# Two groups and an output turned by DMA, sink scores for two groups at once, scores in runs of three pairs, a table built later: one redesign of a windowed attention and its gated feed-forward block

## The chip, the cores and the metric

The kernel runs on one core of one Trainium2 chip. The metric is device microseconds of one execution, the median over several runs. Comparisons are made with runs of the kernel before on the same chip. Ratios are computed as the mean time of one kernel's fast runs over that of the other's fast runs of the same rounds, so a ratio is not quite the ratio of the medians quoted beside it. The profiled span is 1.7 us shorter than the timed one for the kernel before.

## The reference, cut to what matters

Attention of 4 batches, 8 heads, 768 positions, head width 64. Each query sees the last 128 positions and 4 "sink" positions at the start. The result, as 3072 tokens of width 512, goes through a gated feed-forward block of inner width 1536.

```python
keep = is_sink | in_window            # rel in [0, 128), or key < 4
a = softmax(where(keep, q @ k.T / 8, -1e9))
x = (a @ v) as [3072, 512]
g = x @ w_gate
out = (g * sigmoid(g) * (x @ w_val)) @ w_out
```

## The kernel before

The 3072 tokens are 12 groups of 256, three to a batch. For each group, queries and keys must be turned (head width on the partitions) before scores can be computed. Groups 0 to 3 are turned on TensorE (PE) by small matmuls against an identity; the others by the DMA crossbar, out of a loaded tile that is natural in layout.

```python
NPE = 4                               # groups below it are turned by TensorE
def step_T(g, ph): ...                # 32 transposes of 64x64, then two evictions
def cross_T(g):                       # on SyncE's queue
    for j in range(2):
        nc.sync.dma_start(t[:, j]..., nat[g][:, j]..., transpose=True)
```

The attention steps of a group are woven into the feed-forward work of earlier tokens, one unit at a time. A unit is one gate step (4 or 8 matmuls for `pg`, as many for `pv`) or one down tile (12 matmuls into `pd`). `slots` says which attention steps go into which unit. PE is given its instructions in this order; where the next one waits, it stands still. `S` are scores (`s`), `K` the scores against the sinks (`pk`), `PV` the product with the values (`o`), `X` a transpose of the attention output on PE (`px`), `C` a crossbar turn (`kqT`).

```python
def step_K(g):                        # sink scores of one group
    ...
    for p in range(NP2):
        nc.tensor.matmul(ps[KS*p:KS*(p+1)], kss[b][...],
                         queries(g, slice(0, P), p, 0, 2), ...)
us = [g0[0], held g0[2], alone, g0[2], *g1[0:3], g0[3], *g1[3:6], *g0[4:6],
      *downs(0), *g2, *downs(1), *downs(2)]
# ... cuts ...
(9, T(2)), ((10, 11), Ss(2)), (11, [K(2)]), ... (13, C(4)), ...
(15, T(3)), ((16, 17), Ss(3)), ... (18, C(5)), ((20, 21), Ss(4)), (21, [K(4)]),
((22, 22, 23, 23), PVs(4)), (24, Xs(4))
```

Loads are issued by GpSimd, at most eight in flight, in the order of the program: queries, keys, values and weights all share that one queue.

The softmax here doesn't subtract the row's maximum and nothing guards it: scores larger than these inputs give would overflow.

## Time and profile before

| | before |
|---|---|
| median of the timed runs | 245.19 us |
| profiled span | 243.4 us |
| TensorE busy | 96% |
| waits of TensorE for a transfer | none listed |
| first gate matmul | 18.06 us |
| first down matmul | 46.66 us |
| first gate matmul of block 3 | 80.89 us |

"Busy" counts the time in which an engine has an instruction under way; for TensorE, that is close to the whole span. The lines of the page, the waits and the orders of time on which the reasoning rests are in the prediction below. One view it did not look at is VectorE (DVE) in order of time just before the first gate. The columns are start, duration, instruction, and in brackets the idle time before it:

```profile
10.66 0.56 DVE L346 TENSOR_TENSOR e<-e,mask 128x768 bf16<-128x768 bf16 x1 [0.21 <-ACT e L341]
11.42 2.46 DVE L346 TENSOR_TENSOR e<-e,mask 128x768 bf16<-128x768 bf16 x2 [0.21 <-ACT e L341]
```

The same mask product of the same shape takes 0.56 us at 10.66 and 2.46 us for two right after it.

### The profile page before, as it was taken

How to read it: one execution, taken by the hardware profiler on the slowest of the kernel's cores; microseconds unless marked ns; L12 is line 12 of the kernel's file. 1: busy time of each engine (PE TensorE's matmuls, PEld its weight loads, DVE VectorE, ACT ScalarE, POOL GpSimd, SP SyncE). 2: the span in 40 equal slices, each digit the busy share in tenths (PEclk: the TensorE clock that was granted, in tenths of full speed). 3: DMA queues.
4: the chain of work that ended last, by engine and by line, in shares of the span. 5: the costliest groups of instructions: out<-in, count | busy, mean ns of one | idle time of the engine just before them, and what ended most of it. 6: DMA issues, size and time to landing. Idle time of an engine off the chain costs nothing.

```text
span 243.4 us, 5177 instructions
## 1 busy us (share of the span) xinstructions
PE 233.3 (96%) x2060; PEld 136.1 (56%) x2073; DVE 160.6 (66%) x336; ACT 111.2 (46%) x221; POOL 71.1 (29%) x92
## 2 busy tenths in 40 slices
PE   7779999999999999999999999999999999999994
PEld 2557887767755445554455454445454445488443
DVE  2688878929983489890598981399970489878100
ACT  2628637447471274532566512556612562232111
POOL 8985387794276814308000000000000000000000
PEclk9979999999999999999999999999999999999999
DMA  7999999999999999959930335900524200200132
GB/s 138 160 183 198 203 191 203 165 145 171 157 149 159 203 182 117 133 109 134 233 67 1 71 61 141 165 0 1 81 51 129 89 0 0 46 0 3 47 126 88
DMA packets 98792, 27.37 MB, mean 112 GB/s; under 512 B 84816, under 2 KB 95824, under 8 KB 98768
## 3 DMA queue, kind: packets, MB, share of 16 engines
q0 software_dynamic: 68832, 13.90, 70.2%
q1 hardware_dynamic: 29504, 12.75, 26.1%
q10 hardware_dynamic: 432, 0.39, 0.5%
q8 instruction: 16, 0.26, 0.4%
q14 instruction: 8, 0.07, 0.1%
HBM read 28.34 MB, written 6.29 MB: 142 GB/s over the span
## 4 chain that ended last, share of the span: by engine, by line
PE 87%; ACT 5%; DVE 5%; DMA 1%; issue 1%; DVEq 0%; ACTq 0%
PE pv L445 25%; PE pd L498 24%; PE pg L445 23%; PE o L381 5%; PE s L334 3%; ACT e L341 3%; PE pt L270 3%; DVE e L346 2%; PE wm L248 2%; DVE ht L460 1%; PE px L417 1%; DMA out_dram<-ot 1%; ACT xn L389 1%; DVE u L459 1%; ACT kT L275 0%
## 5 line engine op out<-in xcount | busy, mean ns | idle before, releaser
L445 PE MATMUL pv<-xT,wv 128*128 128x256 bf16 (+1 forms) x384 | 74.3, 326 | 0.9 <-DVE ht L460 0.9
L445 PE MATMUL pg<-xT,wg 128*128 128x256 bf16 (+1 forms) x384 | 74.2, 326 | 0.0
L452 ACT ACTIVATE th<-pg 128x512 f32<-128x512 f32 x72 | 43.7, 607 | 60.0 <-PE pg L445 59.4
L459 DVE SCALAR_TENSOR_TENSOR u<-th,pg 128x512 bf16<-128x512 f32 x72 | 49.2, 684 | 30.6 <-ACT th L452 30.1
L498 PE MATMUL pd<-wo,ht 128*128 128x512 bf16 x264 | 62.3, 379 | 0.6
L460 DVE TENSOR_TENSOR ht<-u,pv 128x512 bf16<-128x512 bf16 x72 | 49.5, 688 | 9.5 <-PE pv L445 2.9
L445 PEld LDWEIGHTS <-wg 128*128 128x128 bf16 x384 | 37.4, 98 | 25.4 <-issue 0.2
L341 ACT ACTIVATE e<-s 128x512 bf16<-128x512 f32 (+1 forms) x96 | 46.1, 582 | 0.9 <-PE s L334 0.8
L445 PEld LDWEIGHTS <-wv 128*128 128x128 bf16 x384 | 34.5, 97 | 21.0 <-issue 2.9
L498 PEld LDWEIGHTS <-ht 128*128 128x128 bf16 x276 | 25.8, 98 | 28.0 <-issue 0.2
L502 ACT ACTIVATE ot<-pd 128x512 f32<-128x512 f32 x23 | 13.7, 597 | 53.5 <-PE pd L498 53.5
L346 DVE TENSOR_TENSOR e<-e,mask 128x1024 bf16<-128x1024 bf16 (+1 forms) x48 | 30.4, 671 | 1.1 <-ACT e L341 0.9
L123 POOL DMA_DIRECT2D va<-in_v_dram x24 | 21.3, 894 | 6.0 <-DMA kq<-in_q_dram 3.3
L393 DVE TENSOR_TENSOR xn<-o,rcp 128x256 bf16<-128x256 f32 x46 | 19.5, 425 | 2.8 <-DMA xT<-xn 1.3
L107 POOL DMA_DIRECT2D kq<-in_k_dram x16 | 14.2, 887 | 23.8 <-DMA kqT<-kq 19.8
L381 PEld LDWEIGHTS <-e 128*128 128x128 bf16 x352 | 16.6, 98 | 7.9 <-DVE e L346 2.5
L381 PE MATMUL o<-va,e 128*128 128x65 bf16 x352 | 18.1, 195 | 2.2 <-DVE e L346 2.2
L107 POOL DMA_DIRECT2D kq<-in_q_dram x16 | 14.2, 888 | 6.4 <-DMA va<-in_v_dram 2.8
L386 DVE RECIPROCAL rcp<-o 128x4 f32<-128x4 f32 x48 | 8.4, 176 | 7.2 <-PE o L381 7.2
L275 DVE CAST qT<-pt 128x512 bf16<-128x512 f32 x7 | 4.6, 688 | 9.4 <-PE pt L270 9.4
L483 DVE TENSOR_SCALAR ot<-pd 128x256 f32<-128x256 f32 x1 | 0.4, 425 | 14.4 <-DMA out_dram<-ot 14.4
L381 PE MATMUL o<-vsb,es 128*128 128x260 bf16 x32 | 8.8, 275 | 0.8 <-ACT es L361 0.7
(61 smaller groups left out, 109.4 us busy)
## 6 DMA issues: line engine op xcount, KB each, us to landing
out_dram<-ot SPq DMA_DIRECT2D x23, 256.0 KB
va<-in_v_dram POOLq DMA_DIRECT2D x24, 128.0 KB, 9.1
kq<-in_k_dram POOLq DMA_DIRECT2D x18, 128.0 KB, 8.9
kq<-in_q_dram POOLq DMA_DIRECT2D x16, 128.0 KB, 9.2
wo<-in_moe_w_out_dram POOLq DMA_DIRECT2D x4, 384.0 KB, 12.4
wg<-in_moe_w_gate_dram POOLq DMA_DIRECT2D x4, 256.0 KB, 8.2
wv<-in_moe_w_val_dram POOLq DMA_DIRECT2D x4, 256.0 KB, 8.8
kq<-in_k_dram POOLq DMA_DIRECT2D x3, 256.0 KB, 9.0
```

Source lines behind the costliest of these rows:

```text
L107: nc.gpsimd.dma_start(x[:, j, i].rearrange("p (h d) -> p h d", d=D), src[b, :, t0:t0 + P].rearrange("h m d -> m h d"))
L123: nc.gpsimd.dma_start(va[:, j, :, 0:D], v[b, :, t0:t0 + P].rearrange("h m d -> m h d"))
L341: nc.scalar.activation(e_t[g][:, h0 + h, lo:512], pss[2 * pp + h][:, lo:512], AF.Exp, scale=scale)
L346: nc.vector.tensor_tensor(e, e, m[:, :, lo:512].broadcast_to([P, 2, 512 - lo]), op=ALU.mult)
L381: nc.tensor.matmul(o, l, r, start=(i == 0), stop=(i == len(mms) - 1), skip_group_check=True)
L393: nc.vector.tensor_tensor(xns[g, j][:, 256 * hh:256 * (hh + 1)].rearrange("p (h d) -> p h d", h=4), po[:, :, 0:D], rcp.broadcast_to([P, 4, ...
L445: nc.tensor.matmul(ps[:, i * n:(i + 1) * n], ws[fi][:, c, fo * P:(fo + 1) * P], x[:, 0:n // P, c], start=(c == 0), stop=(c == DMC - 1))
L452: nc.scalar.activation(th, pg, AF.Tanh, scale=0.5)
L459: nc.vector.scalar_tensor_tensor(u, th, 1.0, pg, op0=ALU.add, op1=ALU.mult)
L460: nc.vector.tensor_tensor(hts[tb][:, f:f + two].rearrange("p a n -> p (a n)"), u, pv, op=ALU.mult)
L498: nc.tensor.matmul(po, hts[tb][:, f, ts * P:(ts + 1) * P], wos[f // n][:, f % n], start=(f == 0), stop=(f == DFC - 1))
L502: nc.scalar.activation(ot, po, AF.Copy, scale=0.5)
```

## The change

The intent is to take work off TensorE, which bounds the kernel: turn groups 2 and 3 by the crossbar, turn group 4's attention output by DMA, score three head pairs in one visit to the 64-row form of the array instead of two, compute the sink scores of two groups together, and start the weight loads sooner by building the first sink table after them. The order of units was changed to match (block 1's down tiles before block 2's gates), and turns are issued sooner.

```diff
-    NPE = 4                 # turned by TensorE
-    NXPE = 5                # attention output turned by TensorE
+    NPE = 2
+    NXPE = 3
     load_v(1); load_gate(1)
-    build_vsb(0)
     for i in range(2, 5):
         load_gate(i)
+    build_vsb(0)
 def step_K(g):
+    n = 1 if g < GC else GC - c           # groups from g to the end of its batch
+    for i in range(n):
         ... queries(g + i, ...)
+def S3(ga, gb):                            # eight head pairs of two groups: 3, 3, 2
-    load4(2)
+    load1(2)                               # natural layout, for the crossbar
-    us = [..., *downs(0), *g2, *downs(1), *downs(2)]
+    us = [..., *downs(0), *downs(1), *g2, *downs(2)]
-    (9, T(2)), ((10, 11), Ss(2)), ... (15, T(3)), ((16, 17), Ss(3)), ...
+    (2, C(2)), (8, C(3)), ((11, 12), Ss(2)), (11, [K(2)]), ... (14, C(4)), ... (15, C(5)),
+    ((16, 18, 20), S3(3, 4)), (17, sinks(1)), ((17, 17, 19, 19), PVs(3)), (19, [K(4)]), ...
 # in the later weaves: S3 at s, s+3, s+6; K(7) at unit 1, K(10) at unit 5; turns C(8)..C(11) sooner
```
(Evictions, pool sizes and signatures are left out.)

More of the change, by code (lines that the diff above doesn't have):

```diff
@@ L64 @@
     vpool = pool("vpool", 1)
-    kqtp = pool("kqtp", 3)
+    kqtp = pool("kqtp", 2)
     crossp = pool("crossp", 4)
@@ L317, in step_ks, with step_S @@
                 else cross[b * GC][r, 0, 0, :, 0:NS])
-    def step_S(g, p2):
-        b, c = divmod(g, GC)
-        if p2 == 0:
-            e_t[g] = epool.tile([P, H, 512], BF16, tag="e", name="e")
-        parts = [(2 * c, 0, 2, P), (2 * c + 1, 1, 1, 3 * P)]
-        if c > 0:
-            parts.insert(0, (2 * c - 1, 0, 1, 0))
-        lo = 0 if c > 0 else P
-        pss = [bank([P, 512], FP32, "s") for _ in range(4)]
-        for pp in range(2):
-            p = 2 * p2 + pp
+    def step_S(*pairs):
+        runs = []
+        for g, p in pairs:
+            b, c = divmod(g, GC)
+            if p == 0:
+                e_t[g] = epool.tile([P, H, 512], BF16, tag="e", name="e")
+            parts = [(2 * c, 0, 2, P), (2 * c + 1, 1, 1, 3 * P)]
+            if c > 0:
+                parts.insert(0, (2 * c - 1, 0, 1, 0))
+            pss = [bank([P, 512], FP32, "s") for _ in range(2)]
+            runs.append((g, p, 0 if c > 0 else P, pss))
             for t, j, n, col in parts:
@@ L334, in step_S, with dve @@
                     nc.tensor.matmul(
-                        pss[2 * pp + h][:, col:col + n * P], keys(b, t, r, p),
+                        pss[h][:, col:col + n * P], keys(b, t, r, p),
                         queries(g, r, p, j, n), start=True, stop=True)
-        m = (mask if c > 0 else mask0).rearrange("q (o a) x -> q o (a x)", o=1)
-        for pp in range(2):
-            h0 = 4 * p2 + 2 * pp
+        for g, p, lo, pss in runs:
+            m = (mask if lo == 0 else mask0).rearrange("q (o a) x -> q o (a x)", o=1)
             for h in range(2):
                 nc.scalar.activation(
-                    e_t[g][:, h0 + h, lo:512], pss[2 * pp + h][:, lo:512],
+                    e_t[g][:, 2 * p + h, lo:512], pss[h][:, lo:512],
                     AF.Exp, scale=scale)
-            def dve(e=e_t[g][:, h0:h0 + 2, lo:512]):
+            def dve(e=e_t[g][:, 2 * p:2 * p + 2, lo:512], m=m, lo=lo):
                 nc.vector.tensor_tensor(
@@ L351, in step_K @@
         b, c = divmod(g, GC)
-        if c == 0:
-            return
-        ps = bank([P, 256], FP32, "pk")
-        for p in range(NP2):
-            nc.tensor.matmul(
-                ps[KS * p:KS * (p + 1)], kss[b][:, p * KS:(p + 1) * KS],
-                queries(g, slice(0, P), p, 0, 2), start=True, stop=True)
-        es_t[g] = espool.tile([P, 256], BF16, tag="es", name="es")
-        nc.scalar.activation(es_t[g], ps, AF.Exp, scale=scale)
+        n = 1 if g < GC else GC - c
+        ps = bank([P, n, 256], FP32, "pk")
+        for i in range(n):
+            for p in range(NP2):
+                nc.tensor.matmul(
+                    ps[KS * p:KS * (p + 1), i], kss[b][:, p * KS:(p + 1) * KS],
+                    queries(g + i, slice(0, P), p, 0, 2), start=True, stop=True)
+        es = espool.tile([P, 2, 256], BF16, tag="es", name="es")
+        nc.scalar.activation(es[:, 0:n], ps, AF.Exp, scale=scale)
+        for i in range(n):
+            es_t[g + i] = es[:, i]
     def step_PV(g, j, hh, act=False):
@@ L397, in step_PV @@
         later.append(dve)
-        if hh == 1 and (g >= NXPE or g == 3):
+        if hh == 1 and g >= NXPE:
             later.append(lambda: nc.sync.dma_start(
@@ L531, in Ss @@
     def Ss(g):
-        return [A(step_S, g, p2) for p2 in range(2)]
+        return [A(step_S, (g, p), (g, p + 1)) for p in (0, 2)]
+    def S3(ga, gb):
+        hs = [(ga, p) for p in range(NP2)] + [(gb, p) for p in range(NP2)]
+        return [A(step_S, *hs[i:i + 3]) for i in range(0, 2 * NP2, 3)]
     def PVs(g):
@@ L583 @@
     first_T(1)
-    step_S(0, 0)
+    step_S((0, 0), (0, 1))
     warm(1)
-    step_S(0, 1)
+    step_S((0, 2), (0, 3))
     warm(2)
@@ L600 @@
     step_ks(0)
-    step_S(1, 0)
-    load4(2)
+    step_S((1, 0), (1, 1))
+    load1(2)
     load_v(2)
@@ L621, in first_PVs @@
         later.extend(held)
-    us = [g0[0], (held_gate, 0, 2), (alone, 0, 0), g0[2], *g1[0:3], g0[3], *g1[3:6], *g0[4:6],
-          *downs(0), *g2, *downs(1), *downs(2)]
+    us = [g0[0], (held_gate, 0, 2), (alone, 0, 0), g0[2], *g1[0:3], g0[3], *g1[3:6],
+          *g0[4:6], *downs(0), *downs(1), *g2, *downs(2)]
     weave(us, slots(
-        (0, [flush, A(step_S, 1, 1), K(1), A(next_load, 1)]), (2, [first_PVs]),
-        (3, [A(step_X, 1, 0), A(step_X, 1, 1, True), flush]),
-        (9, T(2)), ((10, 11), Ss(2)), (11, [K(2)]),
-        (12, PVs(2)[:2] + [flush]), (13, PVs(2)[2:] + [flush]), (13, C(4)),
-        (14, [A(step_X, 2, 0), A(step_X, 2, 1, True), flush]),
-        (15, T(3)), ((16, 17), Ss(3)), (17, sinks(1)), ((18, 18, 19, 19), PVs(3)),
-        (18, C(5)), ((20, 21), Ss(4)), (21, [K(4)]),
-        ((22, 22, 23, 23), PVs(4)), (24, Xs(4))))
+        (0, [flush, A(step_S, (1, 2), (1, 3)), K(1), A(next_load, 1)]), (2, [first_PVs]),
+        (2, C(2)), (3, [A(step_X, 1, 0), A(step_X, 1, 1, True), flush]), (8, C(3)),
+        ((11, 12), Ss(2)), (11, [K(2)]), (13, PVs(2)[:2] + [flush]),
+        (14, PVs(2)[2:] + [flush]), (14, C(4)),
+        (15, [A(step_X, 2, 0), A(step_X, 2, 1, True), flush]),
+        (15, C(5)), ((16, 18, 20), S3(3, 4)), (17, sinks(1)), ((17, 17, 19, 19), PVs(3)),
+        (19, [K(4)]), ((21, 21, 22, 22), PVs(4))))
@@ L635, in pair @@
     def pair(ga, gb, sh=0):
         s = sh
-        return [((s, s + 2), Ss(ga)), (s + 2, [K(ga)]),
-                ((s + 4, s + 5, s + 6, s + 7), PVs(ga)),
-                ((s + 6, s + 8), Ss(gb)), (s + 8, [K(gb)]),
+        return [((s, s + 3, s + 6), S3(ga, gb)), ((s + 2, s + 4, s + 5, s + 7), PVs(ga)),
                 ((11, 11, 12, 12) if s else (10, 11, 12, 13), PVs(gb))]
     weave(gates(3) + downs(3), slots(
-        *pair(5, 6, 2), (2, C(6)), (10, C(7))))
-    weave(gates(4) + downs(4), slots((0, sinks(2)), *pair(7, 8), (3, C(8)), (10, C(9)), (14, C(10))))
@@ L645 @@
-    weave(gates(5) + downs(5), slots((0, sinks(3)), *pair(9, 10), (10, C(11))))
+        *pair(5, 6, 2), (2, C(6)), (10, C(7)), (14, C(8))))
+    weave(gates(4) + downs(4), slots(
+        (0, sinks(2)), *pair(7, 8), (1, [K(7)]), (5, C(9)), (10, C(10)), (14, C(11))))
+    weave(gates(5) + downs(5), slots(
+        (0, sinks(3)), *pair(9, 10), (5, [K(10)])))
     weave(gates(6) + gates(7) + downs(6) + downs(7), slots(
-        ((0, 2), Ss(11)), (2, [K(11)]), ((4, 5, 6, 7), PVs(11))))
+        ((0, 2), Ss(11)), ((4, 5, 6, 7), PVs(11))))
```

## The prediction

> **What bounds the kernel now.** I read the page first, then the waits of TensorE, then its instructions in order of time, then the DMA queues in stretches. The page's shares, its tenths in 40 slices (6.1 us each) and its chain:
>
> ```profile
> PE 233.3 (96%) x2060; PEld 136.1 (56%) x2073; DVE 160.6 (66%) x336; ACT 111.2 (46%) x221; POOL 71.1 (29%) x92
> ...
> PE   7779999999999999999999999999999999999994
> ...
> DMA  7999999999999999959930335900524200200132
> ...
> PE 87%; ACT 5%; DVE 5%; DMA 1%; issue 1%; DVEq 0%; ACTq 0%
> ```
>
> TensorE (PE) carries the end: from slice 4 (18 us) on it is never below 90%, and the chain is 87% PE. But the DMA row is just as full in slices 2 to 15, up to about 92 us, and sparse after that. So there are two limits: PE over the whole span, and in the first third a transfer stage which PE happens not to wait for. The waits of PE say so (line, what ended the wait, us in total, times, longest):
>
> ```profile
> PE o L381 <- DVE e L346: 2.2, 3, 1.1
> ...
> PE pv L445 <- DVE ht L460: 0.9, 3, 0.4
> ```
>
> Most of the first stands before 14 us, which the change leaves alone; no DMA is in the list. After 18 us PE stands still for only about 2 us in all, so what the change can gain is PE work, and what it can lose is a wait for DMA that now has none. What a piece of attention costs PE is read from the starts in its order of time (start, duration, instruction):
>
> ```profile
> 35.78 1.04 PE L445 MATMUL pg<-xT,wg 128*128 128x256 bf16 x8
> 36.75 1.09 PE L270 MATMUL pt<-ident,kq 64*64 64x64 bf16 x64
> 37.77 1.05 PE L445 MATMUL pv<-xT,wv 128*128 128x256 bf16 x8
> 38.65 1.04 PE L445 MATMUL pg<-xT,wg 128*128 128x256 bf16 x8
> 39.62 0.61 PE L334 MATMUL s<-qT,kT 64*128 64x128 bf16 x12
> 40.17 1.05 PE L445 MATMUL pv<-xT,wv 128*128 128x256 bf16 x8
> ```
>
> Undisturbed, pg to pv takes 0.87 us (37.77 to 38.65 is such a step). With the 64 transposes of group 2 between them it takes 1.99, so a group's turning costs 1.12. With one score run of two head pairs it takes 40.17 - 38.65 = 1.52, so a run costs 0.65. Its work is 2 x 0.21 (a pair is 512 columns on two half arrays at once; a 512-column matmul takes 0.216), so 0.22 of each run is going into the 64-row form and out of it.
>
> Now the transfers. POOL's queue is q0, the SyncE queue with crossbar turns and stores is q1. First q0 alone (stretch 40 to 52 us), then both (52 to 60 us); packets, MB, share:
>
> ```profile
> q0 software_dynamic: 11305, 1.97, 210.0%
> ```
>
> ```profile
> q0 software_dynamic: 4406, 0.56, 154.4%
> q1 hardware_dynamic: 2145, 0.59, 67.7%
> ```
>
> In the second stretch one group's keys and queries are turned: 2 x 1024 packets of 256 B. q0 with 128 B packets alone runs at about 1190 packets per us (the packets from 50 to 52 us), so 8 us would have carried 9,500; it carried 4,400. The turn thus cost the loads about 4.3 us of transfer. How long it took from its issue shows in SyncE's own order of time:
>
> ```profile
> 49.10 5.13 SPq L304 DMA_TRANSPOSE kqT<-kq  x2
> 54.33 1.10 SPq L504 DMA_DIRECT2D out_dram<-ot  x2
> 55.53 7.98 SPq L304 DMA_TRANSPOSE kqT<-kq  x2
> ```
>
> Its second half was issued as the load landed (50.8), and its last packets went at 59.4: 8.6 us later. The same pair of turns with q0 idle (106.6 to 109.2) took 2.6.
>
> **What the Trainium skill says.** "TensorEngine Tiling (Array Packing)", Key Properties: changing the tiling mode, not merely the tile, drains TensorE. The trace agrees: 0.22 per score run beyond its columns, about 0.11 each way. "DMA: Bandwidth & Descriptors", Queues, rings and completion order: each DMA engine goes round between the rows that have work, packet by packet. The trace agrees in kind: from 61.5 to 67 us q0 and q1 move the same number of packets, about 205 per half us each. Same page, Specifications: below 512 B a transfer is not at line rate. It agrees: 128 B packets land about 155 GB/s in SBUF, 512 and 1024 B ones about 200. Same page, Latency and other measured facts: DMA transposes at 261 GB/s with a non-contiguous middle dimension; here, with q0 idle, about 200.
>
> **The change part by part.**
> Groups 2 and 3 by the crossbar, group 4's attention output too: PE loses 2 x 1.12 = 2.24 us, and 2 x 0.22 = 0.43 for the eight 128-wide transposes of group 4. This is on the path. ACT and DVE lose the evictions (0.59 and 0.69 us each, four apiece); they are off it.
> Scores in runs of three pairs: 24 runs become 20, so 4 x 0.22 = 0.88 off PE.
> Sink scores for two groups at once: before, 8 runs of 0.22 behind a score run (42.57 to 42.79). After, two such runs, and three with twice the columns (0.21) that stand alone and pay both switches (0.22): 1.75 us either way. Nothing.
> First sink table later in POOL's order (1.30 us): loads wait for the landing of the eighth before them, weights land every 1.3 us before and after that instruction, and q0 never runs dry. Nothing.
> PE work removed: 2.24 + 0.43 + 0.88 = 3.55 us, 245.16 to 241.6.
> Added: a run of three takes 6 of 8 PSUM banks and puts six exponentials (0.58 each) in front of ACT's next tanh and es. Working one weave by hand with the trace's durations, es comes about 0.4 late and two banks 0.2 late where before a weave had 0.2 to 0.4 of such waits: about +0.3 each, +0.8 in all.
> Added on DMA: groups 2 and 3 load 128 B packets, four DMAs of 0.9 us in place of two of 1.4, +0.9 each; two turns at about 4.3 each; two smaller turns for group 4. Some 10 us more must pass before group 4 can be used, in the stage where DMA is full.
>
> When is each needed, if PE did not wait? Before, the gates' unit 11 starts at 41.05; without the group 2 transposes and one score run moved behind, at 39.3, and its scores of group 2 at **40.2**. Two units with scores, then four down tiles of 2.6 us with PV and transposes, put the first scores of group 3 at **55.3** and of group 4 at **60.7**.
> When do they arrive? The last weights land at 30.96; then four loads of 0.9: group 2 at 34.4 (before 33.6). Plus 8.6: turned at **43.0**, 2.8 late. If the 1024 B packets of w_out (16 engines, 201 per us) alternate with 256 B ones (590 per us), 150 pairs per us, it is rather 47. w_out itself, 42.9 before, lands at about 48 and is wanted from 44 plus the wait on: just in time.
> Group 3 lands at 45.55 + 1.8 + 4.2 = 51.5, turned at about 60, 4.7 late. Group 4 lands at 50.8 + 1.8 + 8.4 = 61, turned at 69.6, 8.9 late. If turns ran at their own speed and loads gave way, 50.8 + 1.8 + 3 x 3.5 (2048 packets at 590 per us) = 63, and with a start delay like the observed 2.9 us nearer 65: 4 late. These latenesses are not summed; the largest remains, as each pushes PE back and gives the next one time. Later groups have slack: group 5 was turned at 67.4 and used at 85.4.
> So PE waits 4 to 9 us between 40 and 80 us. I take 5, nearer the lower end, because units were moved (down tiles of the next block before gates, turns issued early) by someone who saw this limit. Sum: 245.16 - 3.55 + 0.8 + 5 = 247.4.
>
> **Rivals.**
> (a) The turns arrive in time: 245.16 - 3.55 + 0.8 = 242.4, or 241 if PE's small waits go too. For it: turns alone took 2.6 us, and packets were shared unevenly at times (from 54 to 55 us five to eight to one in favour of q1). Against: q0 is full without a gap to 92 us.
> (b) Turns take strict turns with w_out, and stores and group 4's small turns queue behind group 5's big ones, so gates of block 3 wait as well: 8 to 10 us of waiting, 250 to 251. For it: a store or turn on SyncE's queue took 3 to 4 us to start under load (67.4 to 71.8).
> (c) Three-pair runs starve PSUM: DVE is at 80 to 100% while PE runs gates with scores; if masks come late, each weave could lose 1 to 2 us, 244 to 246 without DMA waits. Against: by hand the banks come free in time.
>
> **Range and chances.** (a) gives the low end, (b) with some of (c) the high end: 242 to 252. Faster by over 2% means under 240.3, below the removed work itself: 0.07. Slower by over 2% needs over 250.1, a wait of about 8 us: 0.23. Within 2%: 0.70.
>
> **What would show it.** PE's transposes 64-wide: 160 in place of 288; score runs 20; PE busy about 4 us less. If right, PE's waits list the crossbar's kqT (or issue gaps before L334 scores) with 4 to 9 us in all between 40 and 65 us. Wrong if PE is at 90% in every slice from 18 us on (then rival a), or if its new waits name exponentials, masks or ht (then c), or xT (then b). The prologue to 18 us should be the same to 0.3 us, and POOL's landing of the weights too; if they land sooner, my zero for the sink table is wrong.

## The result

The changed kernel takes 271.00 us (270.31 to 271.77) against 245.19: ratio 1.107, interval 1.102 to 1.112. It is 10.7% slower, and the result is correct. The forecast was 247.4, within 242 to 252: the direction was right, and the loss was over ten times the one forecast. First the page of the changed kernel: busy shares, the tenths of PE, its granted clock and the DMA engines in 40 slices (6.7 us each), and the chain that ended last.

```profile
PE 238.0 (88%) x1924; PEld 135.9 (51%) x1937; DVE 157.1 (58%) x330; ACT 109.0 (41%) x214; POOL 75.0 (28%) x96
...
PE   7799980999839919999994999999999999999994
...
PEclk9979996699968968999997999999999999999999
DMA  8999999999999999962799114280030410100122
...
PE 52%; DMA 36%; POOL 3%; DVE 3%; issue 2%; ACT 1%; SPq 0%; POOLq 0%; DVEq 0%; ACTq 0%
```

Four holes stand in the PE row: slice 7, slices 11 and 12, slice 15, and slice 22. In or right after each, the clock row drops too. The chain, 1% DMA before, is now 36% DMA. What PE waited for:

```profile
PE s L334 <- DMA kqT<-kq: 8.3, 3, 5.5
PE pk L358 <- DMA kqT<-kq: 7.3, 2, 4.1
PE pg L448 <- DMA xT<-xn: 5.8, 1, 5.8
PE o L384 <- DVE e L345: 1.7, 4, 0.5
```

All three large waits are for transfers, which stood nowhere in this list before. In order of time, each with its idle time in brackets:

```profile
38.03 1.04 PE L448 MATMUL pg<-xT,wg 128*128 128x256 bf16 x8
44.57 0.29 PE L334 MATMUL s<-kqT,kT 64*128 64x128 bf16 x2 [5.50 <-DMA kqT<-kq]
47.31 0.50 PE L334 MATMUL s<-kqT 64*128 64x256 bf16 x4 [2.46 <-DMA kqT<-kq]
...
78.21 0.40 PE L358 MATMUL pk<-kqT,ks 128*32 128x256 bf16 x4 [4.05 <-DMA kqT<-kq]
...
100.09 1.87 PE L448 MATMUL pg<-xT,wg 128*128 128x512 bf16 x4 [5.78 <-DMA xT<-xn]
...
145.08 0.40 PE L358 MATMUL pk<-kqT,ks 128*32 128x256 bf16 x4 [3.25 <-DMA kqT<-kq]
```

The first two are the scores of group 2. The third and the fifth are sink scores: four matmuls for the first group of the pair run, then PE stands until the second group (5, and later 8) has been turned. The fourth is the first gate of block 3, which needs group 4's attention output. They add up to 5.50 + 2.46 + 4.05 + 5.78 + 3.25 = 21.0 us. Note also the 1.87 us of four 512-wide matmuls at 100.09: at full clock such a set takes 1.03.

Where the time went, by the first matmul of each part, from the two traces:

| stretch | before | after | difference |
|---|---|---|---|
| start to first gate | 18.06 | 16.57 | -1.49 |
| to first down tile | 28.60 | 37.01 | +8.41 |
| to block 3's gates | 34.23 | 46.51 | +12.28 |
| to block 4's gates | 35.84 | 37.65 | +1.81 |
| to block 5's gates | 37.24 | 41.74 | +4.50 |
| to the end | 89.45 | 89.55 | +0.10 |

From block 5's gates to the end the kernel is as before to 0.1 us. The loss lies in the stretches with the waits, and 1.81 us in the one to block 4's gates, which has no such wait but begins with work at half clock. The trace has four spells of half clock, each beginning within a wait, with 16.4 us of PE work inside. If half of that is lost, the books nearly close: 21.0 + 8.2 - 3.55 (the work removed) - 1.5 (the start) = 24.2 of 25.6 us.

Why was group 2's turn so late? The DMA queues from 36 to 42 us; columns are packets, MB, share:

```profile
q0 software_dynamic: 971, 0.95, 93.9%
q1 hardware_dynamic: 868, 0.22, 27.6%
```

q0 (loads) carries w_out here, in packets of 1024 B; q1 (the turn) carries 256 B at a time. They move nearly the same number of packets, so the turn gets a fifth of the bytes. Its packets start at 36.3 and end at 46.4 us by the trace: 10 us for what took 2.6 us with an idle q0. It was not issued late: SyncE issued its two halves at 32.38 and 34.06, as their loads landed (32.31 and 34.01).

### The profile page after: what moved, and what is told of

Its sections match the earlier page's. It is cut to its first block, busy times and chain, and to the rows that moved or that the text cites. A ratio compares the mean times of both kernels' runs of the same rounds, so it can differ in the third digit from the quotient of the medians.

```text
span 269.0 us, 4913 instructions
## 1 busy us (share of the span) xinstructions
PE 238.0 (88%) x1924; PEld 135.9 (51%) x1937; DVE 157.1 (58%) x330; ACT 109.0 (41%) x214; POOL 75.0 (28%) x96
## 4 chain that ended last, share of the span: by engine, by line
PE 52%; DMA 36%; POOL 3%; DVE 3%; issue 2%; ACT 1%; SPq 0%; POOLq 0%; DVEq 0%; ACTq 0%
PE pv L448 18%; PE pg L448 17%; DMA kq<-in_q_dram 14%; PE pd L501 13%; DMA kqT<-kq 8%; DMA xT<-xn 5%; DMA wo<-in_moe_w_out_dram 4%; PE o L384 3%; DMA wv<-in_moe_w_val_dram 3%; PE s L334 2%; DMA kq<-in_k_dram 1%; ACT e L340 1%; DVE ht L463 1%; DMA out_dram<-ot 1%; DVE u L462 1%
## 5 line engine op out<-in xcount | busy, mean ns | idle before, releaser
L448 PE MATMUL pg<-xT,wg 128*128 128x256 bf16 (+1 forms) x384 | 78.0, 339 | 5.8 <-DMA xT<-xn 5.8
L448 PE MATMUL pv<-xT,wv 128*128 128x256 bf16 (+1 forms) x384 | 77.7, 337 | 0.1
L455 ACT ACTIVATE th<-pg 128x512 f32<-128x512 f32 x72 | 43.7, 607 | 75.2 <-PE pg L448 72.3
L448 PEld LDWEIGHTS <-wg 128*128 128x128 bf16 x384 | 38.9, 102 | 33.9 <-issue 8.7
L448 PEld LDWEIGHTS <-wv 128*128 128x128 bf16 x384 | 35.4, 100 | 21.9 <-issue 4.7
L107 POOL DMA_DIRECT2D kq<-in_k_dram x20 | 17.9, 893 | 37.9 <-DMA kqT<-kq 31.6
L107 POOL DMA_DIRECT2D kq<-in_q_dram x20 | 17.7, 886 | 6.2 <-DMA kq<-in_q_dram 2.2
L334 PE MATMUL s<-kqT 64*128 64x256 bf16 (+1 forms) x208 | 12.6, 249 | 3.4 <-DMA kqT<-kq 2.8
L334 PEld LDWEIGHTS <-kqT 64*128 64x128 bf16 x208 | 7.6, 98 | 10.3 <-issue 10.0
## 6 DMA issues: line engine op xcount, KB each, us to landing
wo<-in_moe_w_out_dram POOLq DMA_DIRECT2D x4, 384.0 KB, 10.1
```

What stands on the lines that cost most here:

```text
L107: nc.gpsimd.dma_start(x[:, j, i].rearrange("p (h d) -> p h d", d=D), src[b, :, t0:t0 + P].rearrange("h m d -> m h d"))
L334: nc.tensor.matmul(pss[h][:, col:col + n * P], keys(b, t, r, p), queries(g, r, p, j, n), start=True, stop=True)
L448: nc.tensor.matmul(ps[:, i * n:(i + 1) * n], ws[fi][:, c, fo * P:(fo + 1) * P], x[:, 0:n // P, c], start=(c == 0), stop=(c == DMC - 1))
L455: nc.scalar.activation(th, pg, AF.Tanh, scale=0.5)
```

## The experiments

Twelve kernels ran on the chip; all gave correct results. First, three parts of the change, each alone on the kernel before. The order of units, the sink scores of two groups and the DMA for group 4's output were not tried alone on it.

**The sink table alone.**

```diff
-    build_vsb(0)
     for i in range(2, 5):
         load_gate(i)
+    build_vsb(0)
```

> The kernel before with one edit: the first sink table is built on GpSimd behind all weight loads. On record I valued this at zero. The changed kernel's trace shows its first gate matmul at 16.57 us against 18.06 before, and before that two mask products of 1.13 and 1.41 us in place of 0.56 each, at the time when GpSimd builds the table (12.16 to 13.46). Theory: the table's build and VectorE's products slow each other, and moving it gives 1.2 to 1.6 us: 243.7 to 244.0, mask products 0.56 each, first gate matmul near 16.6. Rival: only the weights come sooner, which nobody waits for: 245.2, first gate matmul at 18.0.

Measured: 243.72 us against 244.25, ratio 0.998 (0.995 to 1.001): not clear of zero. The profile of this run shows why both sides of the expectation held something. On its VectorE, in order of time, the two products that were slow in the kernel before are now as short as the others:

```profile
11.20 0.56 DVE L346 TENSOR_TENSOR e<-e,mask 128x768 bf16<-128x768 bf16 x1 [0.21 <-ACT e L341]
11.96 0.56 DVE L346 TENSOR_TENSOR e<-e,mask 128x768 bf16<-128x768 bf16 x1 [0.21 <-ACT e L341]
```

In this run the first gate matmul came at 16.11 us instead of 18.06. But PE then found a new wait, which the kernel before does not have:

```profile
PE pv L445 <- DMA wv<-in_moe_w_val_dram: 1.3, 1, 1.3
```

So 1.3 of the 1.95 us went straight into waiting for the second weight block. Nor are the 1.95 us the table's alone: the slow products explain 1.1 (2.46 us in place of the 1.32 from 11.20 to 12.52), and the kernel before had a half-clock spell of 3.4 us from 14.03, which this run did not have.

**Table late, and group 1's values behind that weight block**, to remove the new wait:

```diff
-    load_v(1)
     load_gate(1)
-    build_vsb(0)
+    load_v(1)
     ...
+    build_vsb(0)
```

> The kernel before with the first sink table behind the weights, as in the run of that alone, and group 1's values loaded behind the second weight block. In that run 1.3 us of the 1.95 gained came back as a wait for the second block's value weights at 21 us. Theory: that wait goes (the block lands 1.7 us sooner, group 1's values about 2.6 later, at 20.3, wanted at 22.5): 242.3 to 242.9, faster than before by 0.6 to 1.0%. Rival: the wait moves to group 1's values or to the third block of weights: 243.5 to 244.

Measured: 243.73 against 244.36, ratio 0.998 (0.995 to 1.002). The wait for weights is gone from the list, but the gain did not grow: this profile has the first gate at 17.25 us, partly because a half-clock spell of 3.4 us (14.5 to 17.9) fell on the work before it, while the profile of the table alone had none there. The expectation of 0.6 to 1.0% fell. The prologue varies by about as much as the edit is worth.

**Runs of three alone**, in the three later weaves, sink scores still per group:

```diff
-    ((s, s + 2), Ss(ga)), (s + 2, [K(ga)]), ((s + 4, ..., s + 7), PVs(ga)),
-    ((s + 6, s + 8), Ss(gb)), (s + 8, [K(gb)]), ...
+    ((s, s + 3, s + 6), S3(ga, gb)), (s + 1, [K(ga)]), (s + 6, [K(gb)]),
+    ((s + 2, s + 4, s + 5, s + 7), PVs(ga)), ...
```

> The kernel before with score runs of three head pairs in the three paired weaves only (groups 5 and 6, 7 and 8, 9 and 10), sink scores still per group, group 8 turned one half weave sooner because its scores come sooner. Theory: three runs fewer at 0.22 us, three sink runs standing alone at +0.11, waits for sink exponentials up to 0.4 each: 244.5 to 246, no wait over 0.6 us. Rival (PSUM starved by six banks at once): waits of 1 to 2 us per weave for masks or exponentials, 248 to 250.

Measured: 248.18 against 244.25, ratio 1.015 (1.011 to 1.019): slower than the theory allowed, and not for the rival's reason. The waits name a transfer, 1.85 us of it for group 6 and 0.89 for group 8:

```profile
PE s L334 <- DMA kqT<-kq: 2.7, 2, 1.8
```

The second run of a weave takes two of its three pairs from the second group, so that group's turned keys are wanted three units sooner.

**The same, with those turns issued sooner** (C(6) during block 2's down tiles, C(7) and C(8) at units 8 and 12 of block 3):

> The run of three-pair score runs alone, with the crossbar turns of groups 6, 7 and 8 issued two to four units sooner. In that run TensorE waited 1.85 and 0.89 us for turned keys (groups 6 and 8), of the 3.9 us by which it was slower. Theory: runs of three lose only because they ask for the second group's turned keys sooner; without those waits 244.0 to 245.5. Rival: ScalarE and PSUM under six exponentials in a row cost the rest, 246 to 247.5, with waits for exponentials or masks of over 0.5 us in each weave.

Measured: 245.84 against 244.91, ratio 1.004 (1.001 to 1.008). No wait for a transfer is left, and the median lies just above the theory's range; no wait of the weaves reaches 0.5 us, so the rival's picture doesn't hold either. Runs of three are thus no gain here, though they save 0.66 us of switching by the prediction's count. What takes it back, sink scores that stand alone or small waits, was not measured apart. Most of the 3.9 us of the run before was transfers asked for too soon.

**The crossbar for groups 2 and 3 alone**, with the order of units of before:

```diff
-    NPE = 4
+    NPE = 2
-    load4(2)
+    load1(2)
-    (9, T(2)), ... (15, T(3)),
+    (2, C(2)), (8, C(3)), ...
```

> The kernel before with groups 2 and 3 turned by the crossbar (turns issued at units 2 and 8 as in the change) and nothing else. Theory: the scores of group 2 are wanted at 38.5 us and the turned keys land at about 47.3 as in the changed kernel: a wait of 8 to 9 us, about 2.5 us more because TensorE's clock is halved after it, less 2.24 of transposes: 253 to 257. Rival: most of the changed kernel's loss comes from the other parts (sink scores of two groups, group 4's output turned by DMA, order of units), then 243 to 248.

Measured: 254.34 against 244.25, ratio 1.042 (1.038 to 1.045), inside the theory's 253 to 257. PE waits 10.6 us for group 2, for its two halves in turn:

```profile
PE s L334 <- DMA kqT<-kq: 10.6, 2, 7.8
```

Groups 3, 4 and 5 are in time in this run: once PE has been held back for group 2, nothing later is late. This is a large part of the loss, but 10 us of nearly 26.

Next, one part undone in the changed kernel.

**Sink scores for one group at a time.**

```diff
-    n = 1 if g < GC else GC - c
+    if c == 0: return                     # as before: one group
-    (1, [K(7)]), ... (5, [K(10)])
+    (s + 1, [K(ga)]), (s + 6, [K(gb)]), ... (2, [K(11)])
```

> The changed kernel with sink scores computed for one group at a time. Theory: computing them for two groups asks for the next group's turned queries too soon; without it the waits of 4.06 us (for group 5) and 3.25 us (for group 8) go, and with them 3.8 us of half-clock work; the wait for group 4's output (5.8) stays: 258 to 263. Rival: the waits only move to the next user of the crossbar (scores of group 8 two units later, group 4's output): 267 to 271.

Measured: 264.54, ratio 1.082 (1.079 to 1.086), against 1.107 of the changed kernel: 6.1 us less (2.5% of 244.3), somewhat less than expected. The waits at `pk` are gone and have not moved to group 8's scores; those for group 2 and for group 4's output have grown a little:

```profile
PE s L334 <- DMA kqT<-kq: 10.1, 3, 6.7
PE pg L444 <- DMA xT<-xn: 6.2, 1, 6.2
```

**Group 4's output by TensorE again.**

```diff
-        if hh == 1 and g >= NXPE:
+        if hh == 1 and (g >= 5 or g == 3):
-    ((21, 21, 22, 22), PVs(4))
+    ((21, 21, 22, 22), PVs(4)), (24, Xs(4))
```

> The changed kernel with group 4's attention output turned by TensorE again (eight 128-wide transposes, 0.43 us). Theory: the wait of 5.78 us before block 3's gates goes, with 1.7 us of half clock after it: 263 to 265. Rival: group 3's output, also turned by DMA behind the turn of group 5, ends the same wait: 268 to 271.

Measured: 266.45, ratio 1.091 (1.087 to 1.094): 4 us less than the changed kernel. The wait for xT is gone, so group 3's output was not what ended it; the rival falls. But the theory's number was too good, because the wait for group 8 grew from 3.25 to 5.15 us:

```profile
PE pk L358 <- DMA kqT<-kq: 9.8, 2, 5.2
```

**Idle matmuls in the waits**, to hold the clock:

```diff
-    ((11, 12), Ss(2)), ...
+    (11, [A(warm, 30)]), ((11, 12), Ss(2)), ...
+    (19, [A(warm, 25), K(4)]), ... warm(22) before block 3 ... (1, [A(warm, 11), K(7)])
```

> The changed kernel with idle 512-column matmuls on zeros put where TensorE waits for a transfer (30 before the scores of group 2, 25 before the sink scores of groups 4 and 5, 22 before block 3's gates, 11 before the sink scores of groups 7 and 8), at most as long as those waits. The result and all transfers stay as they are. Theory: each wait of over 3 us is followed by 3 to 5 us of work at half clock, 8 us lost in all; with TensorE kept at work the clock stays full. The 2.5 us after the first wait are given back in the next wait, which ends with a transfer, so 5 to 6 us are gained: 265 to 266, no half clock between 20 us and the end. Rival: the waits end with transfers that depend on one another alone, so the total stays: 270 to 272, though the clock is full.

Measured: 269.67, ratio 1.106 (1.101 to 1.111), where the changed kernel has 1.107: no difference clear of noise. The clock did what was meant:

```profile
PEclk9979999999999999999999999999999999999999
```

The total lies just under the rival's 270 to 272 and well above the theory's 265 to 266. In this trace block 2's gates start at 64.89 us (66.52 in the changed kernel), 1.6 sooner; block 3's at 99.93 (100.09): what full clock gained before them went into longer waits for transfers. Behind block 3's gates 1.7 us are gained and kept (block 4's gates at 135.91 in place of 137.74), and the profile ends 2.1 us sooner. The intervals of the two ratios leave room for such a gain of up to 2 us, not for 5 to 6. So the 8 us of half-clock work in the books above are real as an account, and at most a quarter of them as a cause.

**w_out loaded behind group 3**, to see what sets the time of a turn:

```diff
     load1(2); load_v(2)
+    load1(3); load_v(3)
     for i in range(4):
         load_out(i)
-    load1(3); load_v(3)
```

> The changed kernel with w_out loaded behind group 3's keys, queries and values, so that the crossbar turn of group 2 shares the DMA engines with packets of 128 B in place of 1024 B. Theory (packets of the two queues take turns one by one, so large ones slow the turn): it lands at about 43 in place of 47.3, the wait before the scores of group 2 falls from 8.0 to 3 to 4.5 us, group 3 is turned sooner too; w_out is perhaps 1 to 3 us late. Total 265 to 269. Rival (a turn takes its time whatever it shares with): landing at 46 to 48, total 270 or more.

Measured: 273.58, ratio 1.120 (1.115 to 1.124): slower still. The waits:

```profile
PE s L334 <- DMA kqT<-kq: 6.9, 3, 2.7
...
PE pd L501 <- DMA wo<-in_moe_w_out_dram: 3.3, 3, 1.8
```

Group 2's turn now shares with 128 B packets. Its packets run from 36.1 to 43.5 us instead of 46.4, and PE waits 5.4 us for it instead of 8.0. Group 3's turn has changed places with it: 7.3 us beside 128 B loads in the changed kernel (52.3 to 59.6), 13.3 here, mostly beside w_out (43.7 to 57.0). So both turns were slower beside the large packets, and a turn does not take its time whatever it shares with. That packets go one for one is another matter: beside 1024 B ones the counts of the two queues agree in each us (156 to 160 of the turn, 154 to 160 of the loads, from 37 to 42 us of the changed kernel), beside 128 B ones they do not (450 to 47 in one us, 53 to 793 in the next). The gain was hoped larger (a wait of 3 to 4.5). The total is worse: w_out is now 3.3 us late, and group 4's turn 1.5. In this stage DMA time was moved about and not found.

**Groups 2 and 3 by TensorE, all other parts kept.**

```diff
-    NPE = 2
+    NPE = 4
-    (2, C(2)), ... (8, C(3)), ... 
+    (9, T(2)), ... (15, T(3)), ...
```

> The changed kernel with groups 2 and 3 turned by TensorE again (2.24 us), all its other parts kept. Theory 1 (each part adds its own wait): 271 less the 10.1 us that the crossbar alone cost: 260 to 262. Theory 2 (the crossbar's transfers make the other waits long): with 10 us less of transfers in the first third, the waits for group 5's turn and group 4's output shrink to 0 to 3 us each and about 3 us remain at group 8's turn: 248 to 254.

Measured: 264.77, ratio 1.081 (1.078 to 1.085). Theory 2, that the other waits are only made long by the crossbar of groups 2 and 3, falls clearly; theory 1 is nearer, but only 6.3 us are gained instead of 10. The waits tell:

```profile
PE pk L358 <- DMA kqT<-kq: 8.7, 2, 4.7
PE pg L448 <- DMA xT<-xn: 5.7, 1, 5.7
```

PE comes to its first down tile 9.8 us sooner than in the changed kernel (43.74 against 53.58) and to block 3's gates only 7.5 sooner (92.57 against 100.09): the sink scores of groups 4 and 5 still wait for group 5 (4.74), group 4's output is as late as ever, and group 8 costs 3.94.

Last, parts undone together.

**Sink scores for one group and group 4's output by TensorE.** The edits are the two shown above.

> The changed kernel with two parts undone: sink scores for one group at a time, group 4's output turned by TensorE; the crossbar for groups 2 and 3 is kept. Theory: what is left is the crossbar's loss as in the run of it alone (254.3), with runs of three and the new order of units on top: 254 to 258, a wait of 8 to 10 us before the scores of group 2 and none over 1.5 us after 60 us. Rival: the two undone parts give only the sum of their single gains in the changed kernel (6.5 and 4.6): 259 to 261.

Measured: 260.02, ratio 1.065 (1.061 to 1.070). The rival's number is right: 2.5 and 1.7 points singly, 4.2 together. The first wait, 7.6 us, is 0.4 short of the theory's; there is one of 2.1 us for group 6 at 103 us, which the theory had ruled out.

**All three undone**: left are the table, the runs of three (also for groups 3 and 4), the order of units and the issue times of turns.

> The changed kernel with three of its parts undone: groups 2 and 3 turned by TensorE, sink scores for one group at a time, group 4's output turned by TensorE. Left are the sink table behind the weights, the runs of three, the order of units and the sooner turns. Theory: the three undone parts hold the whole loss: 243.5 to 246.5, no wait for a transfer over 1 us. Rival: the new order of units (down tiles of block 1 before block 2's gates) or the runs of three cost several us by themselves: 249 or more.

Measured: 249.43 against 244.13, ratio 1.021 (1.017 to 1.026); whether that is over 2% is unclear. It is outside the theory's range and in the rival's: the parts left cost several us by themselves. Runs of three alone cost 1.5 of these 2.1 points, above. The waits for a transfer are those of the runs of three, 1.60 us for group 6 and 1.14 for group 8:

```profile
PE s L334 <- DMA kqT<-kq: 2.7, 2, 1.6
```

One more, 1.06 us of `pd` for `ht`, stands where block 2's gates now run straight into its down tiles, and is new with the order of units.

In points over the kernel before:

| changed kernel with ... | ratio | points taken off |
|---|---|---|
| nothing undone | 1.107 | |
| sink scores one group at a time | 1.082 | 2.5 |
| group 4's output by TensorE | 1.091 | 1.7 |
| groups 2 and 3 by TensorE | 1.081 | 2.6 |
| the first two | 1.065 | 4.2 |
| all three | 1.021 | 8.6 |

The first two add up. The crossbar takes off 2.6 points when undone alone, and 4.4 (1.065 to 1.021) when the other two have gone, which is what it costs alone on the kernel before (4.2). Of the 9.8 us that PE gains at its first down tile by not waiting for group 2, 2.3 are gone by block 3's gates: group 3's transposes (1.12 by the prediction's reading) and longer waits, for group 5's turn by 0.7 and for group 4's by 0.5. After them 1.8 more go: more work of block 3 at half clock, and a wait for group 8 longer by 0.7.

No kernel here beats the one before beyond noise. The two with the table behind the weights are 0.2% faster in the mean with intervals that include zero.

## Why the prediction was wrong

**What held.** The bound was read rightly: PE over the span, DMA in the first third. The turn of group 2 was said to land at 43.0, or 47 if packets alternate with those of w_out; it landed in time for matmuls at 47.3. PE was said to want it at 40.2; its last gate before that was issued at 38.03, so it stood from 39.1. The wait, 8.0 us, was put at 2.8 or, with alternating packets, about 7. The right one of the two mechanisms was not taken for the sum. The counts of instructions are as predicted, too (160 transposes 64 wide, 20 score runs). "These latenesses are not summed; the largest remains" held for groups 3 and 4: after 8.0 us for group 2, they cost nothing and 0.34 us. Two of its signs came out otherwise. PE was busy 4.7 us more, not about 4 less, since matmuls at half clock take longer (1.87 us for a set of 1.03). And a new wait named xT, which it had put down as the sign of rival (b).

**The step that failed in its mechanism** is "Sink scores for two groups at once ... Nothing." It counted columns and switches on PE, and those are right. It did not ask what the instruction needs: the queries of the next group. K(4) in unit 19 wants group 5, which before was first wanted at 85.4 us and here at 74.2, though PE had lost 8 us by then, and which the prediction itself lists as a group with slack. That cost 4.05 us, and for groups 7 and 8 it cost 3.25. Undoing it gave 2.5 points, some 6 us.

**The second** is group 4's output. The prediction took 0.43 us off PE for it and added "two smaller turns" to the transfers; what it waits for appears only in rival (b). Behind the last PV of group 4 (88.1 us) PE had work until 94.3. The turn was issued at 92.92 and took 7.0 us to land (start, duration, what):

```profile
92.92 7.04 DMA xT<-xn
```

The similar turn of group 3 in the kernel before had 12 us from its issue (68.66) to block 3's gates. Undoing it gave 1.7 points, 4 us.

**The third** is the size of the wait in total, "I take 5, nearer the lower end, because units were moved ... by someone who saw this limit". That is trust in an author and no reading of a trace. For the crossbar of groups 2 and 3 it makes 5 - 2.24, some 2.8 us; the run of it alone lost 10.1, the largest miss in microseconds. Together with the two users missed, the waits for transfers were 21.0 us. Two readings under it were off as well: 590 packets of 256 B per us do not fit its own 2.6 us for 2048 of them, which is 790 (turns at that speed would have had group 4 ready at 60.4, in time), and the row of DMA before is full up to slice 17, 103 us, not 15.

**The runs of three** were given -0.88 us for four runs, and +0.8 for waits. Where they could be tested with their turns in time, three weaves with such runs cost 0.4%, about 1 us (0.3 to 1.8), where the two terms sum to nearly nothing. The same runs also want the second group's turn sooner, which cost the difference between 1.015 and 1.004. This was not in the prediction.

**The sink table** was "Nothing", because the weights come no sooner. That held: they come 0.6 to 1.1 us sooner in the profile of the changed kernel (last block at 30.00 instead of 30.96), but the first block, issued before the table, does so too, and in the run of the table alone the last one lands at 30.87. Its sign for the table failed all the same: the prologue was to be the same to 0.3 us, and the first gate came 1.5 us sooner. The gain came from elsewhere: GpSimd built the table from 12.16 to 13.46 us, and two mask products of VectorE around it took 2.46 us instead of 1.32. The Trainium skill has this: "SBUF — State Buffer", Who interferes with whom, says that a VectorE instruction with two SBUF inputs contends with a GpSimd instruction that reads SBUF. The trace agrees: here both were longer (0.56 to 1.12 and 1.41 us, the table 1.30 against 1.07 elsewhere), and in the changed kernel, where the table runs at 17.53, two products of 1024 elements from 17.36 take 2.41, while the table keeps its 1.07. The run of the crossbar alone is a check: its table stands where the kernel before has it, but happened to start at 12.85, behind the products; these took 0.56 each, and the first gate came at 16.61. So it is the overlap that counts. Over the whole kernel moving the table is worth 0.2%, not clear of zero.

**The half clock** was not in the prediction. "TensorE: Matmul & The Clock Gate", Part 1, says that an idle window of about 3.4 us halves the clock. The trace agrees in part. Spells of 10.2, 6.8, 6.8 and 3.4 us, all multiples of 3.41, go with the waits of 8.0, 4.05, 5.78 and 3.25, and begin 2 to 3 us into them. But less idle time than the page's window was enough: the wait of 3.25 us here, and one of 2.06 in the run with two parts undone, with half clock from 104.44 us; the wait of 1.85 us in the run of three-pair runs alone had no spell. Adding those losses in full to the waits would have been a second mistake: with the clock held full, the total did not move clear of noise.

**What stays open.** The last 5 us of the three-undone kernel (1.021) are explained in part: 2.7 us of waits for groups 6 and 8 and 1.06 for `ht`. How much of the remainder is the order of units was not measured alone. That a turn's first packets go about 4 us after its issue when q0 is full was seen three times here (32.38 to 36.3, 48.08 to 52.3, 81.77 to 86.2) and not explained.

## What to carry to other kernels

When work is merged, moved or grouped, write down for every instruction what it now needs and when that is ready; counting its columns on the bounding engine is half of the account. When work goes from a full engine to the DMA queues, look at how full those are in that very stage, and at which packets it will take turns with. Before speeding up the work between two waits, ask whether the second one ends with a transfer: then the gain may only lengthen it.

## What the Trainium skill lacked or had wrong

- "DMA: Bandwidth & Descriptors", Queues, rings and completion order: it says that an engine goes round packet by packet, and gives 9 to 17 descriptors as typical for a packet. It does not say what that does to a small-packet stream beside a large-packet one. Here, in packets as the profile counts them, 256 B turns beside 1024 B loads moved 868 against 971 in 6 us, and a turn of 512 KB took 10.1 us; beside 128 B loads 7.4, with very uneven counts; alone 2.6.
- Same page, DMA Transpose (X-bar), and Latency and other measured facts: no delay from issue to first byte under load is given for a DMA transpose. Here it was 3.9 us (32.38 to 36.3), and a turn of 128 KB took 7.0 us from issue to landing.
- "TensorEngine Tiling (Array Packing)", Key Properties: switching the mode drains the array, without a figure. Here a visit to the 64-row form costs 0.22 us beyond its columns.
- "TensorE: Matmul & The Clock Gate", Part 1: an idle window of about 3.4 us is more than was needed here; waits of 3.25 and 2.06 us were followed by half clock, one of 1.85 was not. No page has that little of its cost may remain where the next wait ends with a transfer: 1.106 with the clock held (1.101 to 1.111), 1.107 without (1.102 to 1.112).
